# Loading the upper half of w_in's rows through GpSimd's DMA queue, with a new order of the opening steps

## The chip, the core and the metric

The kernel runs on one core of a Trainium2 chip. A core has five engines that work side by side, each through its own instructions in order: TensorE (PE, with its weight loads listed as PEld), VectorE (DVE), ScalarE (ACT), GpSimd (POOL) and SyncE (SP). SP computes nothing here; it issues DMAs, which bring data from memory into the on-chip buffer. ACT and POOL can issue DMAs as well. Sixteen DMA engines carry them out. The metric is the device time of one execution in microseconds (us).

## The reference

Two blocks follow each other. The first is a gated linear recurrence with a complex gate for 4 sequences of 768 steps and 8 heads of 48; the second is a two-layer network with an ELU between, on 3072 rows of 384 values and 2048 hidden ones. The weights come as float64, everything else as float32.

```python
mag = np.sqrt(a_re * a_re + a_im * a_im)
scale = np.minimum(mag, 0.999) / (mag + 1e-06)
a_re_n, a_im_n = (a_re * scale, a_im * scale)
for t in range(S):
    ar, ai = (a_re_n[:, :, t, :, None], a_im_n[:, :, t, :, None])
    new_re = ar * S_re - ai * S_im
    new_im = ar * S_im + ai * S_re
    kv = np.einsum('bhd,bhe->bhde', k[:, :, t], v[:, :, t])
    S_re, S_im = (new_re + kv, new_im)
    y[:, :, t] = np.einsum('bhd,bhde->bhe', q[:, :, t], S_re)
...
x = np.ascontiguousarray(attn_out.transpose(0, 2, 1, 3)).reshape(B * S, H * D)
h = x @ w_in
g = np.where(h > 0.0, h, alpha * (np.exp(np.minimum(h, 0.0)) - 1.0))
return (g @ w_out).astype(np.float32)
```

## The kernel before, in words

**Units.** The work is cut into 12 units (u = 0 to 11): 128 steps of two sequences each. A unit goes through the recurrence first, in these steps: the gate's magnitude and angle (`squares` or `squared`, `joined`, `logarithms`, `powers`, `lengths`, `ratios`, `slopes`, `angles`, on ACT and DVE), their sums along time as matmuls (`sums`, `summed`, `decays`, `turns`/`turned`), sines and cosines (`waves`, ACT), the scaling of q and k (`scaled`, `gated`, DVE), transposes on PE with copies on ACT (`transposed`), then `scores`, `states` and `values`, which are matmuls with DVE's masks and state sums and ACT's copies, `ends` (the decay over a whole block), and `seam`, a few small DMAs that move the last rows of the result into the layout of the second block. `noted` is an accuracy check on ACT whose outcome is only read at the very end. The second block then takes the unit as `inner` (x times w_in, two blocks of 128 hidden columns at a time, L1301), `elu` (ACT and DVE) and `project` (times w_out, L1326). Units 0 and 1 run through the plain products; later units use schemes with fewer products.

**Weights.** w_in and w_out stay on chip. Each comes in 8 parts of 768 KB of float64. `fetch` (L659 to 663) issues a part's DMAs on SP into a raw tile; `convert` takes one DVE step of rounding at a time from `rounded` (L665 to 683), four per part, w_in's eight parts first, then w_out's. A w_in part's rows lie on the 128 partitions in two halves: the rows of even heads on partitions 0 to 47 with a rest on 48 to 63, the rows of odd heads on 64 to 111 with a rest on 112 to 127. So a part of w_in is four DMAs (288, 288, 96 and 96 KB, in pieces of 2 KB), a part of w_out one (pieces of 3 KB). The raw tiles of w_in's parts 0 to 3 lie in memory that later holds the hidden values (tags g0 and g1), those of parts 4 to 7 and of all w_out parts in the two w64 buffers, which also hold unit 1's a, q and k. `inner(u, f)` needs part f/2 of w_in rounded, `project(u, n, f0, f1)` w_out's parts up to (f1 - 1)/2.

**Order.** The order of all steps is one list. Its first 329 entries are written out by hand (`first`, from L1745); the rest follows from a plan with due times (`put`, `layer_of`). Steps of the plan that `first` already holds are left out of it. Each step puts its instructions into the queues of the engines in this order, so the list sets every engine's order at once, SP's and POOL's DMA queues too: a DMA that must wait for a tile holds back every later one on its queue. `warm` issues dummy matmuls that keep PE's clock up. `table` loads one of ACT's function tables ahead of use; where a function is not in the table loaded, ACT loads another by itself (lines such as L832). The DMAs of a, q, k and v are at L607 and L611, those of the seam at L1281: for units 0 and 1 POOL issues those of the lower rows (unit 0's last on SP), ACT those of the upper ones (unit 0's last on SP). `carry_on` (L879) is a small DMA on POOL that hands a unit's last angle on; it waits for the turns.

**DVE's convert steps** (L671, L674, L677, L679): two cheap ones, two dearer.

Of the kernel before, what the change touches and what calls it, by code (L numbers as in the profile page):

```python
# [505 lines left out]
def kernel(  # L506
# [128 lines left out]
    def weights_of(kind, m):  # L635

        if kind == "in":
            n = WF * DM // NI
            dst, cols = w_in[:, :, ts(m, n)], ts(m, 2 * n)
            tag = "g" + str(m // 2) if m < 4 else "w64"  # L640
            t = sb.tile([C, WF * DM, 2], U32, tag=tag, bufs=2, name="w64")
# [1097 lines left out]
    def gates_of(u, *at):  # L1739
# [30 lines left out]
        (begun, 2), (squares, 2), (fetch, "out", 3), (joined, 2), (elu, 1, 6), *2 * [(convert,)], (elu, 1, 0), (convert,), (elu, 1, 2), *2 * [(convert,)], (elu, 1, 4),  # L1770
        (logarithms, 2), (inner, 1, 12), (load_a, 3), (convert,), (inner, 1, 8),
        (fetch, "out", 4), (inner, 0, 10), (inner, 0, 14), (elu, 1, 12), (inner, 0, 12), (convert,), (fetch, "out", 5), (convert,), (noted, 2), *2 * [(convert,)], (load_v, 2), (powers, 2),
        (elu, 1, 8), (convert,), (elu, 0, 10), (convert,), (ratios, 2),
        *2 * [(convert,)], (elu, 0, 14), (inner, 1, 10), *2 * [(convert,)], (elu, 0, 12),
        (convert,), (elu, 1, 10), *3 * [(convert,)], (load_qk, 2), (convert,), (fetch, "out", 6),
# [170 lines left out]
```

## Time and profile before

| what | value |
|---|---|
| median of 3 runs | 619.08 us (618.47 to 620.57) |
| profiled execution, its own time | 621.27 us |
| span of that execution, first to last instruction | 619.5 us |
| mean granted clock of PE | 0.997 |
| moved by DMA | 65.54 MB, of it q1 (SP's queue) 62.72 MB, q0 (POOL's) 1.20 MB |
| w_in's DMAs, issue to landing, median | 5.8 us (288 KB), 5.7 us (96 KB) |
| w_out's parts, issue to landing, median | 4.7 us (768 KB) |

The profile is a page on one execution. It lists the busy time of each engine, the span in 40 equal slices with the busy share of each in tenths, the DMA queues, and groups of instructions. A digit 9 is 90% or more. Further views of the same trace are used below: busy time of all engines in stretches of time, the waits of an engine by what ended them, and the instructions of one engine in order of time, where a bracket at the end gives the idle time before an instruction and what ended it. Several equal instructions in a row are merged into one line with their number, and then the duration is that of the group.

### The profile page before, as it was taken

What the parts mean: (1) busy time and instruction counts of PE and PEld (TensorE: products, weight loads), DVE (VectorE), ACT (ScalarE), POOL (GpSimd) and SP (SyncE); (2) the same over time, 40 slices, a digit from 0 to 9 for tenths busy, and PEclk for the clock granted to TensorE, in tenths of its full rate; (3) what the DMA queues carried; (4) which work ended last, traced back from release to release, by engine and by line L of the source; (5) the groups of instructions that cost most, each with busy time, mean ns of one, the idle gap of its engine ahead of it and who ended that gap; (6) DMA issues with size and microseconds to landing.
All of it is one profiled execution on the core that took longest, in us unless ns stands there. A gap on an engine that the chain in (4) does not pass through costs nothing. (4 is left out here: it accounts for less than half of the span.)

```text
span 619.5 us, 16960 instructions
## 1 busy us (share of the span) xinstructions
PE 605.0 (98%) x6980; PEld 550.0 (89%) x6980; DVE 503.0 (81%) x781; ACT 415.8 (67%) x681; POOL 176.5 (28%) x240
## 2 busy tenths in 40 slices
PE   8799999999999999999999999999999999999996
PEld 6678887567899999999999999999999999999996
DVE  5788878667599899888898898899898888984482
ACT  5975674675787667776777876777777777661350
POOL 2000100103113534523524434534534422422000
PEclk9989999999999999999999999999999999999999
DMA  9978739630653253746556545546673647342101
GB/s 165 183 139 136 152 111 239 145 65 22 91 90 58 53 97 81 143 95 123 118 104 123 118 103 121 125 99 122 126 134 85 142 80 132 73 87 66 53 2 32
DMA packets 192179, 65.54 MB, mean 106 GB/s; under 512 B 168116, under 2 KB 181596, under 8 KB 192092
## 3 DMA queue, kind: packets, MB, share of 16 engines
q1 hardware_dynamic: 187920, 62.72, 51.6%
q0 software_dynamic: 3520, 1.20, 1.7%
q8 instruction: 57, 0.93, 0.7%
q10 hardware_dynamic: 652, 0.44, 0.3%
q14 instruction: 30, 0.25, 0.2%
HBM read 48.91 MB, written 4.80 MB: 87 GB/s over the span
## 5 line engine op out<-in xcount | busy, mean ns | idle before, releaser
L1410 PE MATMUL mlp<-w_out,g 128*128 128x192 f32 x640 | 112.1, 328 | 0.0
L1410 PEld LDWEIGHTS mlp<-w_out,g 128*128 128x128 f32 x640 | 104.3, 190 | 3.3 <-DVE ee L1424 0.6
L1132 POOL TENSOR_TENSOR S<-S,T 128x384 f32<-128x384 f32 x36 | 38.0, 1057 | 150.0 <-DVE S L1130 83.1
L1388 DVE TENSOR_TENSOR g<-g 128x512 f32<-128x512 f32 x80 | 60.7, 774 | 6.3 <-PE mlp L1410 4.7
L1301 PE MATMUL mlp<-x,w_in 128*128 128x256 f32 x288 | 64.1, 381 | 0.0
L1301 PEld LDWEIGHTS mlp<-x,w_in 128*128 128x128 f32 x288 | 54.7, 192 | 8.5 <-issue 0.6
L1569 ACT ACTIVATE ee<-g 128x512 f32<-128x512 f32 x63 | 39.6, 629 | 29.5 <-DVE g L1564 26.8
L1548 PE MATMUL mlp<-x,w_in 128*128 128x128 f32 x424 | 56.3, 276 | 0.1
L1410 PE MATMUL mlp<-w,g 128*128 128x192 f32 x320 | 54.5, 329 | 0.0
L1410 PEld LDWEIGHTS mlp<-w,g 128*128 128x128 f32 x320 | 51.8, 190 | 0.6
L1548 PEld LDWEIGHTS mlp<-x,w_in 128*128 128x128 f32 x424 | 51.7, 192 | 0.6 <-DVE g L1564 0.3
L1281 POOL DMA_DIRECT2D x<-y x62 | 30.6, 499 | 72.2 <-ACT y L1177 40.4
L1570 ACT ACTIVATE ee<-ee 128x512 f32<-128x512 f32 x72 | 45.4, 631 | 2.3
L1573 DVE SCALAR_TENSOR_TENSOR g<-ee,g 128x512 f32<-128x512 f32 x63 | 42.4, 682 | 2.3 <-ACT ee L1570 2.3
L1561 ACT COPY g<-mlp 128x512 f32<-128x512 f32 x36 | 20.9, 584 | 29.4 <-PE mlp L1548 29.4
L1564 DVE TENSOR_TENSOR g<-g,mlp 128x512 f32<-128x512 f32 x45 | 30.8, 684 | 8.9 <-PE mlp L1548 4.1
L1291 ACT ACT_TABLE_LOAD x24 | 30.8, 1283 | 2.1 <-issue 1.6
L921 ACT ACTIVATE n<-w 64x384 f32<-64x384 f32 (+1 forms) x60 | 28.1, 486 | 5.2 <-PE w L906 4.4
L1548 PE MATMUL mlp<-x,g 128*128 128x128 f32 x224 | 30.1, 277 | 0.0
L1268 ACT COPY x<-y 128x384 f32<-128x384 f32 x20 | 8.6, 482 | 30.9 <-PE y L1160 30.9
L1075 POOL COPY qt<-kt 32x512 f32<-32x512 f32 x24 | 24.4, 1017 | 16.3 <-PE mlp L1548 10.2
L1548 PE MATMUL y<-x,w_in 128*128 128x128 f32 x216 | 28.5, 275 | 0.0
(218 smaller groups left out, 1369.7 us busy)
## 6 DMA issues: line engine op xcount, KB each, us to landing
w<-in_moe_w_out_dram SPq DMA_DIRECT2D x8, 768.0 KB, 4.7
g<-in_moe_w_in_dram SPq DMA_DIRECT2D x24, 256.0 KB, 3.1
g<-in_moe_w_out_dram SPq DMA_DIRECT2D x24, 256.0 KB, 3.0
w<-in_moe_w_in_dram SPq DMA_DIRECT2D x16, 288.0 KB, 5.8
vn<-in_v_dram SPq DMA_DIRECT2D x24, 192.0 KB, 5.6
qt<-kt SPq DMA_DIRECT2D x72, 64.0 KB, 2.0
kt<-cs SPq DMA_DIRECT2D x72, 64.0 KB, 2.3
q<-in_q_dram SPq DMA_DIRECT2D x11, 384.0 KB, 4.7
```

Of the source, the lines that this page charges most:

```text
L921: nc.scalar.activation(out=flat(x[key][to, n : n + 1]), in_=t[of], func=AF.Exp, scale=sign)
L1132: eng.tensor_tensor(out=new_s, in0=new_s, in1=wide, op=ALU.mult)
L1281: eng.dma_start(out=x["x"][ds(j * HP + D, G), i], in_=x["y"][ds(j * HP + i * G, G)])
L1291: nc.scalar.preload_act_table_set(name)
L1301: nc.tensor.matmul(t[:, e], lhsT=w_in[:, i, ts(f + e, C)], rhs=x["x"][:, i], start=(i == 0), stop=(i == NI - 1),)
L1388: nc.vector.tensor_tensor(out=S_of(u, k, h), in0=a, in1=b, op=op)
L1410: nc.tensor.matmul(to, lhsT=a[:, m], rhs=b[:, m], start=(first and h == 0 and m == 0), stop=False, skip_group_check=True,)
L1548: nc.tensor.matmul(x["c" + c][:, ts(m, C)], lhsT=a[:, m], rhs=x["mix"][p], start=(p == BANKS[c][0] and m == 0), stop=False, skip_group_che ...
L1564: nc.vector.tensor_tensor(out=part(u, to), in0=part(u, a), in1=part(u, b), op=op)
L1569: nc.scalar.activation(out=e, in_=part(u, of), func=AF.Relu, scale=-1.0)
L1570: nc.scalar.activation(out=e, in_=e, func=AF.Exp, scale=-1.0)
L1573: nc.vector.scalar_tensor_tensor(out=part(u, to), in0=nat[u]["e", to], scalar=-1.0, in1=part(u, of), op0=ALU.add, op1=ALU.max,)
```

## The change

It has three parts. The DMAs of w_in's upper rows (partitions 64 to 127) leave `fetch` and are issued by a new step, `fetch_far`, on POOL's queue. The raw tiles of w_in's parts 4 to 7 move from the w64 buffers into the tile of w_out, 4 blocks of 384 columns each, which holds nothing until the first part of w_out is rounded. And the written-out list is made anew: it has the same steps as often as before, the eight `fetch_far` steps besides, in another order. Of the list the diff shows here the beginning, as far as the first `inner` steps of unit 1.

```diff
@@ -637,8 +637,11 @@
         if kind == "in":
             n = WF * DM // NI
             dst, cols = w_in[:, :, ts(m, n)], ts(m, 2 * n)
-            tag = "g" + str(m // 2) if m < 4 else "w64"
-            t = sb.tile([C, WF * DM, 2], U32, tag=tag, bufs=2, name="w64")
+            if m < 4:
+                t = sb.tile([C, WF * DM, 2], U32, tag="g" + str(m // 2), bufs=2, name="w64")
+            else:
+                t = w_out[:, ts(m - 4, 2 * WF)].rearrange("p f n -> p (f n)").bitcast(U32)
+                t = t.rearrange("p (n two) -> p n two", two=2)
             words = t.rearrange("p (i n) two -> p i (n two)", i=NI)
             pairs = []
             for j in range(2):
@@ -658,13 +661,18 @@
 
     def fetch(kind, m):
         t, dst, pairs = weights_of(kind, m)
-        for to, of in pairs:
+        raw[kind, m] = t, dst, pairs[1::2]
+        for to, of in pairs[::2]:
             nc.sync.dma_start(out=to, in_=of)
-        raw[kind, m] = t, dst
+
+    def fetch_far(m):
+
+        for to, of in raw["in", m][2]:
+            nc.gpsimd.dma_start(out=to, in_=of)
 
     def rounded(kind, m):
 
-        w, dst = raw.pop((kind, m))
+        w, dst, _ = raw.pop((kind, m))
         lo, hi = w[:, :, 0], w[:, :, 1]
         f = sb.tile([C, WF * DM], U32, tag="wt", bufs=2, name="wf")
         r = sb.tile([C, WF * DM], U32, tag="wt", bufs=2, name="wr")
@@ -1743,54 +1751,68 @@
 
 
     first = [
-        (warm, 1), (warm, 12), (fetch, "in", 0), (begun, 0), (inverses, 0), (inverses, 1),
-        (load_qk, 0), (squared, "ar", 0), (squared, "ar", 1), (squared, "ai", 0),
-        (squared, "ai", 1), (joined, 0, 0), (logarithms, 0, 0), (joined, 0, 1), (logarithms, 0, 1),
-        (lengths, 0, 0), (ratios, 0, 0), (lengths, 0, 1), (powers, 0, 0), (sums, 1), (sums, 0),
-        (warm, 2), (powers, 0, 1), (ratios, 0, 1), *2 * [(convert,)], (table, "trig_and_small", 0),
-        (load_a, 1), (fetch, "in", 1), (load_v, 0), (angles, 0, 0), (fetch, "in", 2),
-        (angles, 0, 1), (summed, 0), (warm, 1), (decayed, 0, 0), (convert,), (summed, 1), (turned, 0, 0), (turned, 0, 1), (decayed, 0, 1), (waves, 0, 0), (waves, 0, 1),
-        (begun, 1), (table, "natural_log_exp_and_others", 0), (ends, 0), (scaled, 0, "q", 0),
-        (warm, 2), (warm, 1), (scaled, 0, "k", 0), (gated, 0, 0), (scaled, 0, "q", 1),
-        *2 * [(warm, 1)], (scaled, 0, "k", 1), (warm, 1), (squares, 1), (transposed, 0, "q", 0),
-        (transposed, 0, "k", 0), (convert,), (gated, 0, 1), (joined, 1), (transposed, 0, "q", 1),
-        *2 * [(convert,)], (load_qk, 1), (scores, 0, 0), (logarithms, 1), (states, 0, 0),
-        (powers, 1), (transposed, 0, "k", 1), (lengths, 1), (convert,), (ratios, 1), (convert,), (slopes, 1), (warm, 2), (noted, 1), (values, 0, 0), (decays, 1), (warm, 2), (scores, 0, 1),
-        (states, 0, 1), (angles, 1), *2 * [(warm, 2)], (scaled, 1), (noted, 0), (values, 0, 1),
-        (carry_on, 0), (fetch, "in", 3), (convert,), (ends, 1), (convert,), (seam, 0),
-        (load_v, 1), (table, "trig_and_small", 1), (convert,), (warm, 1), (turns, 1), (convert,), (waves, 1), (inner, 0, 2), (inner, 0, 0), (fetch, "in", 4), (load_a, 2), (fetch, "in", 5),
-        (table, "natural_log_exp_and_others", 1), (gated, 1, 0), (convert,), (gated, 1, 1),
-        (convert,), (elu, 0, 2), (transposed, 1, "q", 0), (transposed, 1, "k", 0),
-        (convert,), (transposed, 1, "q", 1), (scores, 1, 0), (convert,), (states, 1, 0),
-        (inner, 0, 4), *2 * [(convert,)], (transposed, 1, "k", 1), (convert,), (warm, 4),
-        (scores, 1, 1), (values, 1, 0), (fetch, "in", 6), (convert,), (fetch, "in", 7),
-        (states, 1, 1), (convert,), (elu, 0, 0), (convert,), (elu, 0, 4), (values, 1, 1),
-        (seam, 1), *2 * [(convert,)], (inner, 0, 8), (inner, 0, 6), (convert,), (elu, 0, 8),
-        (convert,), (inner, 1, 6), (inner, 1, 0), (fetch, "out", 0), (convert,), (inner, 1, 2), (elu, 0, 6), (convert,), (inner, 1, 4), (fetch, "out", 1), (fetch, "out", 2),
...
+        (begun, 0), (squared, "ar", 0), (squared, "ai", 0), (warm, 12), (joined, 0, 0),
+        (squared, "ar", 1), (squared, "ai", 1), (fetch, "in", 0), (load_qk, 0), (logarithms, 0, 0),
+        (inverses, 0), (ratios, 0, 0), (joined, 0, 1), (logarithms, 0, 1), (warm, 2), (inverses, 1),
+        (ratios, 0, 1), (fetch_far, 0), (lengths, 0, 1), (load_a, 1), (sums, 1), (angles, 0, 0),
+        (convert,), (angles, 0, 1), (lengths, 0, 0), (fetch, "in", 1), (powers, 0, 1), (convert,),
+        (powers, 0, 0), *2 * [(warm, 1)], (convert,), (turned, 0, 0), (turned, 0, 1), (load_v, 0),
+        (sums, 0), (begun, 1), (convert,), (warm, 2), (summed, 0), (fetch_far, 1), (decayed, 0, 0),
+        (summed, 1), (fetch, "in", 4), (decayed, 0, 1), (scaled, 0, "k", 0), (waves, 0, 0),
+        (scaled, 0, "q", 0), (warm, 1), (scaled, 0, "q", 1), (ends, 0), (waves, 0, 1),
+        (gated, 0, 0), (warm, 1), (begun, 2), (warm, 1), (scaled, 0, "k", 1), (warm, 1),
+        (squares, 1), (warm, 2), (gated, 0, 1), (transposed, 0, "q", 0), (fetch, "in", 2),
+        (load_qk, 1), (transposed, 0, "k", 0), (carry_on, 0), (transposed, 0, "q", 1), (convert,),
+        (joined, 1), (states, 0, 0), (convert,), (table, "natural_log_exp_and_others", 0),
+        (logarithms, 1), (convert,), (transposed, 0, "k", 1), (opened,), (convert,), (powers, 1),
+        (scores, 0, 0), (lengths, 1), (states, 0, 1), (warm, 2), (scores, 0, 1), (ratios, 1),
+        (fetch_far, 2), (noted, 1), (fetch, "in", 3), (convert,), (slopes, 1), (values, 0, 0),
+        (warm, 1), (decays, 1), (values, 0, 1), (table, "trig_and_small", 0), (warm, 2),
+        (fetch, "out", 0), (angles, 1), (seam, 0), (convert,), (ends, 1), (fetch, "in", 6),
+        (warm, 2), (scaled, 1), (turns, 1), (convert,), (load_qk, 2), (convert,), (waves, 1),
+        (gated, 1, 0), (load_v, 1), (fetch_far, 3), (inner, 0, 2), (inner, 0, 0), (fetch, "in", 5),
+        (elu, 0, 2), (transposed, 1, "q", 0), (gated, 1, 1), (transposed, 1, "k", 0),
+        (fetch_far, 4), (warm, 4), (load_a, 2), (fetch_far, 6), *2 * [(convert,)],
+        (transposed, 1, "q", 1), (begun, 3), (convert,), (scores, 1, 0), (states, 1, 0),
+        (fetch_far, 5), (inner, 0, 4), (convert,), (noted, 0), (convert,), (transposed, 1, "k", 1),
+        *2 * [(convert,)], (values, 1, 0), (convert,), (begun, 4), (elu, 0, 0),
+        (table, "natural_log_exp_and_others", 3), (scores, 1, 1), (squares, 2), (fetch, "in", 7),
+        *2 * [(convert,)], (states, 1, 1), (elu, 0, 4), (inner, 0, 8), (fetch_far, 7),
+        (values, 1, 1), (fetch, "out", 1), (joined, 2), (inner, 0, 6), (convert,), (seam, 1),
+        (inner, 1, 6), (convert,), (elu, 0, 8), (inner, 1, 0), (elu, 0, 6), *2 * [(convert,)],
...
```

In the rest of the new list, unit 2's gate steps come ahead of several of units 0 and 1's `inner` and `project` steps, and the last `convert` steps, the sums of weights for the later scheme (`combined`, `summed_in`) and unit 3's steps stand in a new order. `opened`, which only names buffers, stands much earlier.

More of the change, by code (lines that the diff above doesn't have):

```diff
@@ L1772 @@
[L1772 to L1775, printed above, removed]
-        (project, 1, 0, 0, 4), (convert,), (inner, 1, 14), (slopes, 2), *2 * [(convert,)], (project, 1, 1, 0, 4), (project, 0, 0, 0, 4), (angles, 2), (lengths, 2), (fetch, "out", 7),
@@ L1777 @@
-        (project, 0, 0, 4, 8), (elu, 1, 14), (project, 0, 1, 0, 4), (convert,), (decays, 2),
-        (project, 1, 0, 4, 8), (carried, 2), (convert,), (table, "trig_and_small", 2),
-        *2 * [(convert,)], (turns, 2), (waves, 2), (convert,), (table, "natural_log_exp_and_others", 2), (scaled, 2), (project, 0, 1, 4, 8), (convert,), (begun, 3), (table, "trig_and_small", 3), (project, 0, 1, 8, 12), (convert,), (project, 1, 1, 4, 8), (squares, 3), (gated, 2), (project, 1, 0, 8, 12), *2 * [(convert,)], (joined, 3), (convert,), (transposed, 2, "k", 1), (transposed, 2, "q", 1), (table, "natural_log_exp_and_others", 3), (convert,), (ends, 2), (convert,), (logarithms, 3), (project, 1, 1, 8, 12), (powers, 3), (load_qk, 3), (transposed, 2, "k", 0),
@@ L1780 @@
-        (convert,), (ratios, 3), (convert,), (lengths, 3), (project, 1, 0, 12, 16), (slopes, 3),
-        (transposed, 2, "q", 0), (project, 1, 1, 12, 16), (angles, 3), (scored, 2),
-        (opened,), (states, 2, 0), (valued, 2), *3 * [(convert,)], (seam, 2),
-        (project, 0, 0, 8, 12), (combined, 1, 1), (summed_in, 0), (noted, 3), (carried, 3),
-        (summed_in, 1), (combined, 2, 1), (combined, 4, 1), (combined, 1, 0), (summed_in, 4),
-        (summed_in, 2), (project, 0, 1, 12, 16), (combined, 2, 0), (turns, 3), (combined, 4, 0),
@@ L1786 @@
-        (inner, 2, 4), (inner, 2, 6), (load_a, 4), (ends, 3), (inner, 2, 2), (load_v, 3),
-        (inner, 2, 0), (elu, 2, 4), (scaled, 3), (elu, 2, 6), (summed_in, 3), (elu, 2, 2),
-        (waves, 3), (gated, 3, None, ("k",)), (elu, 2, 0), (gated, 3, None, ("q",)),
-        (project, 0, 0, 12, 16), (inner, 2, 10), (transposed, 3, "k", 0), (warm, 2), (begun, 4),
-        (folded, 2, 0, (3, 1)), (load_v, 4), (inner, 2, 8), (summed_in, 7), (squares, 4),
-        (elu, 2, 10), (load_qk, 4), (transposed, 3, "q", 0), (transposed, 3, "q", 1),
@@ new lines @@
+        (inner, 1, 6), (convert,), (elu, 0, 8), (inner, 1, 0), (elu, 0, 6), *2 * [(convert,)],
+        (load_a, 3), (convert,), (inner, 1, 2), (logarithms, 2), (convert,), (powers, 2),
+        (elu, 1, 6), (convert,), (inner, 1, 4), (convert,), (inner, 1, 12), (elu, 1, 0),
+        (inner, 1, 8), (ratios, 2), (elu, 1, 2), (convert,),
+        (table, "natural_log_exp_and_others", 1), (lengths, 2), (noted, 2), *2 * [(convert,)],
+        (elu, 1, 12), (elu, 1, 4), (slopes, 2), *2 * [(convert,)], (fetch, "out", 2), (convert,),
@@ new lines @@
+        (inner, 0, 14), (elu, 1, 8), (load_v, 2), *2 * [(convert,)], (inner, 0, 10), (angles, 2),
+        (convert,), (fetch, "out", 3), (elu, 0, 14), (convert,), (decays, 2), (inner, 0, 12),
+        (convert,), (fetch, "out", 4), (inner, 1, 14), (fetch, "out", 5), (project, 1, 0, 0, 4),
+        (carried, 2), (scaled, 2), (elu, 0, 10), *5 * [(convert,)], (squares, 3), (fetch, "out", 6),
+        *2 * [(convert,)], (ends, 2), (joined, 3), (turns, 2), (project, 1, 1, 0, 4),
+        *2 * [(convert,)], (fetch, "out", 7), (table, "natural_log_exp_and_others", 2),
@@ new lines @@
+        *2 * [(convert,)], (inner, 1, 10), (convert,), (elu, 1, 10), (logarithms, 3), (convert,),
+        (elu, 0, 12), (convert,), (waves, 2), (load_v, 3), (convert,), (project, 1, 1, 4, 8),
+        (gated, 2), (convert,), (project, 1, 0, 4, 8), (table, "trig_and_small", 2), (convert,),
+        (elu, 1, 14), (project, 0, 0, 0, 4), (project, 0, 1, 0, 4), (convert,),
+        (transposed, 2, "k", 1), (convert,), (project, 0, 1, 4, 8), (convert,),
+        (transposed, 2, "q", 1), (convert,), (transposed, 2, "k", 0), (convert,), (combined, 1, 0),
@@ new lines @@
+        (project, 1, 0, 8, 12), (summed_in, 1), (powers, 3), (ratios, 3), (convert,),
+        (project, 0, 1, 8, 12), (convert,), (slopes, 3), (project, 1, 0, 12, 16), (summed_in, 0),
+        (transposed, 2, "q", 0), (project, 1, 1, 8, 12), (noted, 3), (load_a, 4),
+        (project, 1, 1, 12, 16), (lengths, 3), (load_qk, 3), (angles, 3), (convert,), (scored, 2),
+        (project, 0, 1, 12, 16), (states, 2, 0), (valued, 2), (seam, 2), (load_v, 4), (carried, 3),
+        (project, 0, 0, 4, 8), (turns, 3), (inner, 2, 6), (inner, 2, 4), (inner, 2, 0), (elu, 2, 6),
@@ new lines @@
+        (elu, 2, 4), (scaled, 3), (waves, 3), (project, 0, 0, 8, 12), (summed_in, 3),
+        (combined, 2, 0), (combined, 4, 0), (elu, 2, 0), (gated, 3, None, ("q",)), (ends, 3),
+        (convert,), (project, 0, 0, 12, 16), (squares, 4), (gated, 3, None, ("k",)),
+        (combined, 3, 0), (inner, 2, 2), (inner, 2, 8), (table, "trig_and_small", 3), (warm, 2),
+        (summed_in, 4), (load_qk, 4), (elu, 2, 2), (combined, 1, 1), (transposed, 3, "k", 0),
+        (summed_in, 6), (convert,), (combined, 2, 1), (summed_in, 2), (inner, 2, 10),
@@ L1794 @@
+        (combined, 4, 1), (table, "trig_and_small", 1), (summed_in, 5), (transposed, 3, "q", 0),
+        (inner, 2, 12), (folded, 2, 0, (3, 1)), (elu, 2, 10), (convert,), (combined, 3, 1),
+        (transposed, 3, "q", 1), (summed_in, 8), (joined, 4), (elu, 2, 8), (transposed, 3, "k", 1),
+        (summed_in, 7),
     ]
```

4 lines of the change are left out of this document (removed).

## The prediction

> **What bounds the kernel now.** I read the profile's page first, then busy time by stretches, then what TensorE (PE) waited for.
>
> ```profile
> span 619.5 us, 16960 instructions
> PE 605.0 (98%) x6980; PEld 550.0 (89%) x6980; DVE 503.0 (81%) x781; ACT 415.8 (67%) x681; POOL 176.5 (28%) x240
> ...
> PE   8799999999999999999999999999999999999996
> ```
> ```profile
> 0.00:65.00 65.00, 57.94 (x778) 48.47 (x778) 49.26 (x74) 47.32 (x87) 5.92 (x34) 0.97 0.94 153
> 65.00:140.00 75.00, 75.00 (x395) 55.22 (x392) 57.44 (x78) 48.37 (x78) 4.06 (x6) 1.00 0.63 144
> ```
> ```profile
> 42.00:44.00 2.00, 2.00 (x5) 1.39 (x6) 1.61 (x3) 1.36 (x2) 0.00 (x0) 0.50 0.65 130
> ```
> ```profile
> PE w L1034 <- ACT qt L1038: 1.8, 1, 1.8
> PE mlp L889 <- DVE n L793: 1.1, 1, 1.1
> PE w L970 <- DVE once L968: 0.7, 2, 0.4
> PE w L963 <- ACT n L937: 0.7, 1, 0.7
> ```
>
> In the stretch rows the columns are PE, weight loads, DVE, ACT, POOL, then the granted PE clock, the DMA share and GB/s. PE bounds the kernel: 605.0 of 619.5 us. Of the 14.5 us in which it idles, 65.00 - 57.94 = 7.1 lie in the first 65 us, none between 65 and 140. The list that the change makes anew governs this opening. It holds the same steps as before with the same number of dummy matmuls (37 in both; I counted), so PE's work is the same and the change can only move PE's waits and the stretch at half clock (0.50 between 42 and 44). There is no line of a DMA among PE's longest waits: the opening is a chain through ACT and DVE, where DMA is a supplier that has so far been in time. What can be won is at most the waits after the first loads, some 5 us, and the half-clock stretch; what can be lost has no such cap.
>
> **ACT's queue.** In these rows the columns are start, duration, engine, line, operation.
>
> ```profile
> 21.37 1.28 ACT L1291 ACT_TABLE_LOAD   x1
> ...
> 35.44 1.28 ACT L832 ACT_TABLE_LOAD   x1
> ...
> 37.48 0.92 ACT L816 ACTIVATE n<-n,most_sq 128x768 f32<-128x768 f32 x1
> ...
> 39.46 0.72 ACT L1172 COPY x<-y 128x192 f32<-128x192 f32 x2
> ...
> 40.45 1.50 ACTq L1281 DMA_DIRECT2D x<-y  x2
> 41.98 1.28 ACT L1291 ACT_TABLE_LOAD   x1 [1.56 <-issue]
> 43.91 0.58 ACT L859 ACTIVATE n<-w,magic 128x384 f32<-128x384 f32 x1 [0.64 <-PE w L854]
> ```
>
> Unit 0's chain up to its waves has in both lists the same ACT steps and two table loads in it; angles now come ahead of powers, which swaps the loads and adds none. I let it end at 21.37 as before. Then, before: a load (1.28), 12.8 us of work up to 35.44 (squares to decays of unit 1), a load for the angles, the angles (36.72 to 37.48), noted(0) from 37.48 to 39.46, the copies of values(0, 1) 1.0, two DMA issues 1.5, another load, and the turns' first step at 43.91. New: the load moves behind squares and three pairs of copies but stays in the stretch: 21.4 + 1.3 + 12.8 = 35.5; copies 1.0, one load that serves angles and waves, 1.28: ACT is ready for the angles at 37.8. Gone from this stretch are noted(0), 2.0, which the new list puts behind states(1, 0), and one load, 1.28.
>
> **DVE's queue**, which must finish slopes(1) ahead of those angles.
>
> ```profile
> 23.14 0.95 DVE L679 SCALAR_TENSOR_TENSOR w_in<-w,wf 128x768 uint32<-128x768 uint32 x1
> ...
> 24.88 0.96 DVE L1020 TENSOR_TENSOR kg<-k,cs 128x768 f32<-128x768 f32 x1
> ...
> 26.62 0.56 DVE L671 TENSOR_SCALAR wr<-w 128x768 uint32<-128x768 uint32 x1
> ...
> 29.40 0.56 DVE L1128 TENSOR_TENSOR S<-mlp,T 128x384 f32<-128x384 f32 x1 [1.14 <-PE mlp L1115]
> ...
> 34.73 0.95 DVE L679 SCALAR_TENSOR_TENSOR w_in<-w,wf 128x768 uint32<-128x768 uint32 x1
> 35.60 0.95 DVE L807 SCALAR_TENSOR_TENSOR n<-n 128x768 f32<-128x768 f32 x1
> 36.47 0.68 DVE L1087 TENSOR_TENSOR a<-w,mask 128x512 f32<-128x512 f32 x1
> 37.23 0.56 DVE L1128 TENSOR_TENSOR S<-mlp,T 128x384 f32<-128x384 f32 x1
> ```
>
> Full tiles follow each other by 0.87 (34.73, 35.60, 36.47), cheap convert steps cost about 0.5. Before, gated(0, 1) ended at 24.88 + 0.87 = 25.8. The new list does part 0's last convert step (the row at 23.14) earlier, in an idle stretch, so 24.9. From there to the end of slopes(1) it has: part 1's four convert steps 2.8, one of part 2 0.5, joined, lengths and slopes 3 x 0.87 = 2.6, ratios 1.8, two masks 2 x 0.6, two sets of three state sums 2 x 1.7, and the wait for PE's state products, 1.2 as in the row at 29.40: 13.5, so 38.4. Before it was 36.47: scores(0, 1), states(0, 1) and a convert step now stand ahead of it. So angles(1) runs from 38.4 instead of 36.7, but behind it ACT has only the two DMA issues: 38.4 + 0.75 + 1.5 = 40.7, and with some 0.5 for the handovers the turns' first step at 41.2, 2.7 earlier than 43.91.
>
> **PE, and what then is late.**
>
> ```profile
> 42.38 2.77 PE L854 MATMUL w<-n,sum_turns 128*128 128x384 f32 x4
> 44.95 5.59 PE L1301 MATMUL mlp<-x,w_in 128*128 128x256 f32 x24
> ...
> 54.27 1.15 PE L1115 MATMUL w<-vn,kg 64*64 64x48 f32 x64
> ...
> 65.04 31.35 PE L1301 MATMUL mlp<-x,w_in 128*128 128x256 f32 x144
> ```
> ```profile
> x<-y ACTq DMA_DIRECT2D x2, 16.0 KB, 2.3
> ```
>
> The first inner(0, 2) follows the turns on PE directly before (44.95). In the new list the turns' matmuls are through at about 41, and inner(0, 2) needs unit 0's seam, whose last DMA ACT issues behind the angles, at about 40.2 to 41.2; with 2.3 to landing that is 43.5. So PE idles some 2.5 us on a DMA, a wait that is not there now, and starts 44.95 - 43.5 = 1.45 earlier. The 24 matmuls at 44.95 took 5.59 where the rate of the row at 65.04 gives 24 x 0.218 = 5.2: 0.4 of half clock, which I count as gone here. From there to states(1, 0) I find no new PE wait on ACT or DVE. The four dummy matmuls move ahead of it (0.9), neither gain nor loss in the end. Part 3 to 7's conversions stand with as much PE work ahead of their users as before, and noted(0), now at about 55, waits there beside long inner steps, where ACT has room; without that cover it would cost its 2.0. Between 65 and 140 PE never waited, so steps moved within that stretch count nothing; DVE's 57.44 of 75 us is the cover.
>
> Whether the clock falls again is open. The Trainium skill, page "TensorE: Matmul & The Clock Gate", section on the HAM clock gate, has it fall to half after an idle window of about 3.4 us, by which 2.5 us would not do it. The trace disagrees: the clock was at 0.50 from 42 on with no wait of PE longer than 1.8. So I bound it: a stretch of the same length at the new wait costs nothing against before; none gains up to 1.7 (3.4 us at half speed, an estimate from the row of 42 to 44); a second one loses 1.7. I take the middle.
>
> **The fetches.**
>
> ```profile
> 1.93 1.85 SPq L607 DMA_DIRECT2D ai<-in_a_im_dram  x2
> ...
> 41.72 1.38 SPq L607 DMA_DIRECT2D vn<-in_v_dram  x2
> ```
> ```profile
> 4.42 0.14 POOL L1625 MEMSET seen<- 128x60 f32 x1
> ```
> ```profile
> L974 POOL DMA_DIRECT2D T<-ends x20: 938/954/1002, 119.5 to 533.5; - x20
> ```
> ```profile
> vn<-in_v_dram SPq DMA_DIRECT2D x2, 192.0 KB, 4.5
> ```
> ```profile
> 10.00:20.00 10.00, 7.85 (x60) 5.44 (x59) 5.76 (x15) 9.49 (x16) 0.65 (x1) 1.00 1.34 188
> ```
> ```profile
> DMA packets 412, 0.75 MB, mean 186 GB/s; under 512 B 48, under 2 KB 48, under 8 KB 412
> ...
> q1 hardware_dynamic: 412, 0.75, 93.7%
> ```
> ```profile
> DMA packets 260, 0.75 MB, mean 300 GB/s; under 512 B 16, under 2 KB 16, under 8 KB 260
> ...
> q1 hardware_dynamic: 260, 0.75, 74.9%
> ```
>
> The last two pairs are 70 to 74 us, when w_in's halves were moving, and 75.5 to 78, with w_out's 128-row tiles: 0.75 MB cost 4.0 x 0.937 = 3.7 us of all engines for w_in and 2.5 x 0.749 = 1.9 for w_out. A w_in half of 384 KB thus holds the engines 2.0 us when sent alone, and 1.0 if halves sent together reach w_out's pace. The Trainium skill, page "DMA: Bandwidth & Descriptors", section "Rules for kernel authors", says of two transfers to disjoint partition halves: don't bother, they serialize; by it a half stays at 2.0. The rows above show w_in's slow pace but no two halves together.
>
> On SP each fetch loses two of its four issues. On POOL a fetch_far is two issues of at most 0.95 each (the row of L974, its dearest). Parts 0 and 1 wait for nothing and go out once POOL's set-up ends (4.42), when ai's issue is over (3.8): they can hold up a, q, k by 0 to 2 x 2.0 = 4.0, less the 2.0 that SP's own queue lost; I take 0. Parts 3 to 7 stand behind seam(0) and the carry of turns(1) on POOL, so they go out from about 43.5 on, five halves within some 6 us. Beside them SP loads unit 1's v, which the new list puts behind part 6's lower half and unit 2's q and k. Before, v went out at 41.72 and landed by 46.2, 8 us before states(1, 0) at 54.27. New: SP is free of the seam some 2.6 earlier, but ahead of v stand 2.0 and 786 KB at 188 GB/s = 4.2, so 49.8 alone; needed at 54.27 - 1.45 - 0.4 + 0.9 = 53.3. A margin of 3.5 against 1.0 to 2.0 for each half that gets in front: I take 0.3 for it, since only some do.
>
> **Sum**: -1.45 - 0.4 + 0.3 = -1.5 of the span of 619.5; the profiled execution's own 621.27 goes to 619.8, and as the median of the runs stands 2.2 under it, 617.6.
>
> **Rivals.** 1. *The opening shrinks by more*: the seam lands before the turns are through, so all 2.7 of the earlier turns count, and the half-clock stretch vanishes: -2.7 - 1.7 - 0.3 = -4.7, 614.4. For it: ACT loses 3.3 us of steps; against it: DVE's slopes come 2 us later. 2. *Slower, through unit 1's v*: nothing holds POOL's five halves back and they take the engines ahead of v, 5 to 10 us. It costs from 3.5 on; at five halves and 1.5 each v comes 4.0 late, PE stands at states(1, 0) (inner(0, 4) and all else queued behind), and the sum is -1.8 + 4.0 = +2.2, 621.3; at 2.0 each 623.7. That is where the skill's rule on halves would lead. Against it: SP's share of the engines goes on beside POOL's. 3. *No effect*: the wait for the seam brings a longer half-clock stretch that eats 1.7: 619.2.
>
> **Numbers.** Forecast 0.42, rival 1 0.20, rival 2 0.22, rival 3 0.16. About 0.3% (1.9 us) is what a measurement can tell from no change. The forecast lies just inside it and goes out to either side of that line by its unknown terms, half of it each: faster 0.20 + 0.21 = 0.41; slower the most of rival 2 and a little of 3, 0.23; the same 0.36. The range, 614.6 to 621.4, runs from rival 1 to rival 2's middle.
>
> **What would show it.** Right: ACT's turns step near 41 and one table load fewer before it; PE waiting 2 to 3 us for x's DMA ahead of L1301 near 43.5; the long run of L1301 shifted by 1 to 2 us. Rival 2: a PE wait of over 2 us at L1115 near 54 whose releaser is vn's DMA. Rival 1: no wait ahead of L1301. Wrong altogether: PE waits between 65 and 140, or DVE waiting for a raw part.

## The result and the profile after

The new kernel is slower: 635.79 us as the median of 4 runs (634.97 to 641.03) beside 619.83 us for the kernel before on the same chip (4 runs, 618.47 to 621.16). The ratio is 1.0272, with a 95% interval from 1.022 to 1.0324. The forecast was 617.6 with a range from 614.6 to 621.4. One execution of e5 below took 2168.23 us, the other five 624.83 to 632.81; that one is left out there, as of a slow state.

The page of the new kernel, in the rows that the prediction showed of the old one, with the granted clock and the DMA share by slices added; below it the clock of the kernel before:

```profile
span 634.2 us, 16962 instructions
PE 610.9 (96%) x6980; PEld 553.7 (87%) x6980; DVE 502.3 (79%) x781; ACT 423.7 (67%) x686; POOL 186.7 (29%) x256
...
PE   7798699999999999999999999999999999999996
...
PEclk9889699999999999999999999999999999999999
DMA  9989906637230334853945646646656656242101
```
```profile
PEclk9989999999999999999999999999999999999999
```

The span grew by 14.7 us (the profiled execution of the kernel before was one of 621.27 us, 2.2 above its median, so the medians differ by 16.0). PE idles 634.2 - 610.9 = 23.3 instead of 14.5, so 8.8 are new waits. The other 5.9 are PE's busy time (610.9 against 605.0) for the same 6980 matmuls, and the PEclk row tells why: it drops in the 2nd, 3rd and 5th slice, where the kernel before had a drop in the 3rd alone. Nearly all of both lies in the first five slices of 16 us: 8.2 of the 8.8 us of waits stand before 140 us.

Busy time by stretches (PE, weight loads, DVE, ACT, POOL, granted PE clock, DMA share, GB/s), first the two that the prediction showed, then one cut out:

```profile
0.00:65.00 65.00, 54.77 (x586) 45.81 (x586) 45.36 (x68) 43.21 (x77) 14.61 (x50) 0.95 1.07 166
65.00:140.00 75.00, 69.94 (x457) 52.86 (x455) 59.71 (x82) 52.13 (x82) 4.09 (x6) 0.93 0.55 124
```
```profile
69.20:79.20 10.00, 6.72 (x82) 5.50 (x79) 3.90 (x7) 5.07 (x7) 0.00 (x0) 0.50 1.02 196
```

Where PE never waited before (65 to 140) it now idles 5.1 us, and up to 65 it idles 3.2 more. The second fence holds the longest of three stretches at half clock (0.50): 10 us, in which PE was busy for 6.72 with work worth half of that. The other two, of 3.4 us each, begin at about 21.3 and 31.6. Together that is 17.1 us at half clock, where the profile before has 3.4.

PE's waits in the first 320 us, longest sums first (in total, times, longest):

```profile
PE mlp L1123 <- DMA vn<-in_v_dram: 3.0, 1, 3.0
PE w L1123 <- DMA vn<-in_v_dram: 2.4, 2, 1.3
PE w L1123 <- issue: 2.2, 1, 2.2
...
PE y L1159 <- issue: 1.8, 1, 1.8
```

The list before had no DMA in it; now one stands on top. v is late twice, once for unit 0 and once for unit 1. The chain of waits between 18 and 82 us shows how late (start, duration, what):

```profile
20.56 9.24 DMA vn<-in_v_dram
...
51.69 18.85 DMA vn<-in_v_dram
...
70.67 1.96 PE w L1123 x62
72.63 2.16 issue
```

Before, unit 0's v had landed 7.5 us after its issue and unit 1's 4.5; now it took 9.24 and 18.85. What stood beside the second one is in GpSimd's timeline, five upper halves within 8 us, and in the DMA rows of the wait itself, 51.7 to 70.5 us (packets, MB, share):

```profile
50.23 1.14 POOL L671 DMA_DIRECT2D w<-in_moe_w_in_dram  x2
51.36 2.76 POOL L671 DMA_DIRECT2D w_out<-in_moe_w_in_dram  x5
...
56.92 1.21 POOL L671 DMA_DIRECT2D w_out<-in_moe_w_in_dram  x2 [1.65 <-DMA w<-in_moe_w_in_dram]
```
```profile
q0 software_dynamic: 752, 1.97, 64.8%
q1 hardware_dynamic: 4213, 1.14, 50.1%
```

q0 is GpSimd's queue and q1 SP's. The percentages are the share that a queue's packets take of all 16 engines' time: 64.8 + 50.1 = 115, no room is left. GpSimd's 1.97 MB are all five halves (5 x 384 KB): every one of them moved while the second of v's two DMAs was under way. (18.85 - 4.5) / 5 = 2.9 us is what each upper half cost v, if the whole delay is theirs; by the time of the engines that they took it is 0.648 x 18.8 / 5 = 2.4.

Was the room there before? The DMA share answers it, and this is the reading that the prediction lacked. First three stretches of the kernel before, then the same of the new one:

```profile
8.00:20.00 12.00, 9.85 (x66) 6.55 (x65) 7.04 (x16) 10.47 (x18) 0.65 (x1) 1.00 1.30 186
20.00:30.00 10.00, 7.67 (x104) 6.70 (x103) 8.82 (x14) 9.94 (x16) 0.00 (x0) 1.00 1.11 181
30.00:40.00 10.00, 9.75 (x193) 8.29 (x191) 9.65 (x14) 9.80 (x23) 0.00 (x0) 1.00 0.97 152
```
```profile
8.00:20.00 12.00, 9.74 (x65) 6.50 (x63) 7.90 (x14) 9.36 (x16) 1.60 (x3) 1.00 1.28 172
20.00:30.00 10.00, 6.16 (x39) 5.68 (x40) 6.29 (x11) 9.25 (x16) 0.00 (x0) 0.83 1.20 182
30.00:40.00 10.00, 10.00 (x184) 9.10 (x186) 7.65 (x13) 5.46 (x10) 0.00 (x0) 0.83 1.02 158
```

The share sums the time that packets are under way on the 16 engines; packets of one engine overlap, so it can pass 1. In the kernel before it stands at about 1 or more from 8 to 40 us: the engines always held work, and the loads were still in time; that this rests on SP's one queue, which sends them in the order of need, is what e2 below tests. The second queue moved no more per second: 186, 181, 152 GB/s before, 172, 182, 158 after, and 182, 186, 181 with the new list on one queue (e1 below).

### The profile page after: what moved, and what is told of

Same layout as the page of the kernel before. It is cut to its first block, busy times and chain, and to the rows that moved or that the text cites. A ratio compares the mean times of both kernels' runs of the same rounds, so it can differ in the third digit from the quotient of the medians.

```text
span 634.2 us, 16962 instructions
## 1 busy us (share of the span) xinstructions
PE 610.9 (96%) x6980; PEld 553.7 (87%) x6980; DVE 502.3 (79%) x781; ACT 423.7 (67%) x686; POOL 186.7 (29%) x256
## 4 chain that ended last, share of the span: by engine, by line
PE 84%; DMA 7%; SPq 4%; DVE 3%; issue 1%; ACT 1%; DVEq 0%; ACTq 0%
PE mlp L1418 27%; PE mlp L1556 15%; PE mlp L1309 9%; PE y L1556 8%; DMA vn<-in_v_dram 4%; PE w L1123 4%; PE mlp L1334 3%; PE y L1334 3%; PE y L1168 3%; PE y L1238 3%; SPq L611 2%; PE y L1159 2%; PE w L862 2%; PE w L1042 1%; PE w L914 1%
## 5 line engine op out<-in xcount | busy, mean ns | idle before, releaser
L1309 PE MATMUL mlp<-x,w_in 128*128 128x256 f32 x288 | 67.2, 390 | 0.9 <-DMA x<-y 0.7
L1138 DVE TENSOR_TENSOR S<-w,S 128x384 f32<-128x384 f32 x38 | 20.9, 553 | 15.8 <-PE w L1123 14.5
L1123 PEld LDWEIGHTS w<-vn,kg 64*64 64x64 f32 x1280 | 23.5, 139 | 8.6 <-issue 5.9
L1123 PE MATMUL w<-vn,kg 64*64 64x48 f32 x1280 | 26.2, 225 | 4.6 <-DMA vn<-in_v_dram 2.4
L1320 DVE SCALAR_TENSOR_TENSOR g<-ee,mlp 128x512 f32<-128x512 f32 x24 | 16.4, 684 | 16.8 <-ACT ee L1319 16.8
```

Of the source, the lines that this page charges most:

```text
L1123: nc.tensor.matmul(to, lhsT=of, rhs=vn[u % 2][ts(c, L), n, ts(h, D)], start=True, stop=True,)
L1309: nc.tensor.matmul(t[:, e], lhsT=w_in[:, i, ts(f + e, C)], rhs=x["x"][:, i], start=(i == 0), stop=(i == NI - 1),)
```

## The experiments

Two theories. **Engines full**: w_in's narrow halves keep all DMA engines busy in the opening; a second queue adds no speed, only takes the order away, so something needed sooner lands later. **New list**: the new order of the compute steps is itself the harm, and the queue is a side matter. The runs compare with medians of the kernel before on their own chips: 620.32 (e1 to e4), 619.08 (e5 to e8) and 619.47 us (e9 to e12).

**e1, the new list on one queue.**

```diff
-        raw[kind, m] = t, dst, pairs[1::2]
-        for to, of in pairs[::2]:
+        raw[kind, m] = t, dst, []
+        for to, of in pairs:
```


> The new list and the raw tiles in w_out stay; each fetch issues all four DMAs of a part on SP again and the far steps issue nothing. Queue theory (POOL's halves take the DMA engines from a, v and the instruction loads): the waits for vn's DMA and for instructions shrink and most of the 14.7 us of span comes back, under 624 us. List theory (the new list itself puts too much to load ahead of v): unit 0's v still has parts 0, 1 and 4 ahead of it, now whole ones on the same queue, so the wait at states(0, 0) stays at 3 us or grows, and the time stays at 632 or more.

Measured: 629.02 us, ratio 1.0156 [1.0135, 1.0176]. So the queue is worth 635.79 - 629.02 = 6.8 on this list, and 8.7 remain. Both theories have a share, and the time lies between what either expected. v is nearly in time here (PE waits 0.2 for it), but the seams are not: SP issues the last DMAs of unit 0's seam behind its loads, and this issue takes 4.63 us. The first row is from PE's waits, of which two, 2.9 in all, stand at unit 0's seam and one, 2.3, at unit 1's; the second is from SP's timeline.

```profile
PE mlp L1309 <- DMA x<-y: 5.2, 3, 2.3
```
```profile
41.12 4.63 SPq L1289 DMA_DIRECT2D x<-y  x2
```

**e2, the old list with the second queue**, the upper halves issued on GpSimd where `fetch` stands; raw tiles as before.

```diff
-        for to, of in pairs:
-            nc.sync.dma_start(out=to, in_=of)
+        for n, (to, of) in enumerate(pairs):
+            eng = nc.gpsimd if n % 2 else nc.sync
+            eng.dma_start(out=to, in_=of)
```


> The list and the raw tiles of before; of each w_in part the two DMAs of the upper rows go out on POOL's queue at the place of the fetch. Queue theory: the old opening, which never waits for a DMA after the first loads, gets such waits: 5 us or more slower than before. List theory: it stays within 2 us of before. If halves on two queues really moved side by side, parts would land earlier and the time would not rise at all.

Measured: 638.15 us, 1.0321 [1.0283, 1.0359]: 18 us for the queue alone. PE's waits, ACT's wait, and GpSimd's timeline:

```profile
PE mlp L1302 <- DMA x<-y: 6.0, 1, 6.0
PE w L1035 <- ACT qt L1039: 5.6, 1, 5.6
PE w L1035 <- DVE qg L1021: 2.4, 1, 2.4
```
```profile
27.37 0.84 ACT L737 ACTIVATE n<-w 128x768 f32<-128x768 f32 x1 [5.09 <-DMA w<-in_a_re_dram]
```
```profile
4.51 3.45 POOL L663 DMA_DIRECT2D w<-in_moe_w_in_dram  x6
...
75.06 0.59 POOL L663 DMA_DIRECT2D w<-in_moe_w_in_dram  x1 [5.43 <-DVE w_in L680]
76.67 1.55 POOL L1282 DMA_DIRECT2D x<-y  x3
```

Two things happen. At 4.5 us GpSimd sends the upper halves of parts 0, 1 and 2 at once, while SP still has q, k and unit 1's a to send; a lands late, ACT's squares wait 5.09, and PE waits for ACT's copies, which stand behind the squares on ACT's queue. Later GpSimd itself stands 5.43 us for a raw buffer that DVE's conversion must free, and the seam of unit 1 is queued behind that: PE's 6.0.

**e3, the raw tiles in w_out alone**, old list, one queue.

```diff
-            tag = "g" + str(m // 2) if m < 4 else "w64"
-            t = sb.tile([C, WF * DM, 2], U32, tag=tag, bufs=2, name="w64")
+            if m < 4:
+                t = sb.tile([C, WF * DM, 2], U32, tag="g" + str(m // 2), bufs=2, name="w64")
+            else:
+                t = w_out[:, ts(m - 4, 2 * WF)].rearrange("p f n -> p (f n)").bitcast(U32)
+                t = t.rearrange("p (n two) -> p n two", two=2)
```


> The list and the one queue of before; only the raw tiles of parts 4 to 7 lie in w_out's unused space. All theories: SP waits less for buffers (21.8 us before) and PE waits as before, so within 1.5 us of before. If this place of the raw tiles costs something by itself, it shows here alone.

Measured: 620.39 us (10 runs), 1.0011 [0.9984, 1.0039]. This part costs nothing.

**e4, v ahead of the loads it waited behind**, in the new kernel.

```diff
-(load_a, 1), (sums, 1)
+(load_a, 1), (load_v, 0), (sums, 1)
...
-(convert,), (load_qk, 2), (convert,), (waves, 1),
+(convert,), (load_v, 1), (load_qk, 2), (convert,), (waves, 1),
```


> The changed kernel with only the v loads of units 0 and 1 moved up in the list: unit 0's directly behind unit 1's a, unit 1's ahead of unit 2's q and k. If the late v is what costs, PE's waits for vn (3.0, 1.3 and 1.1 us) go, and with them part of the half-clock time: 5 to 9 us less than the changed kernel, 627 to 631. If the engines are simply short of time in the opening, the waits move to the next loads (part 1, unit 1's q and k) and the time stays within 2 us of 635.8.

Measured: 638.28 us, 1.0321 [1.0286, 1.0357]. v's waits are gone, and PE idles 635.7 - 617.7 = 18.0 us, 5.3 less than in the new kernel. But its busy time rose by 6.8, from 610.9 to 617.7, which takes more than that away; the first row is the page's, the second PE's longest wait:

```profile
PE 617.7 (97%) x6980; PEld 557.8 (88%) x6980; DVE 502.0 (79%) x781; ACT 423.5 (67%) x686; POOL 187.0 (29%) x256
```
```profile
PE y L1159 <- issue: 3.0, 1, 3.0
```

The clock stands at half for 30.7 us in this profile, 17.1 in the new kernel's. So the waits did not simply move to other loads, as the second case of the expectation had it: 5.3 us of waits were won, and lost again to the clock. Why the clock falls more often here is not shown.

A wait whose releaser is "issue" has no cause in the profile. The two longest of the new kernel (1.8 and 2.2, between 65 and 75 us) lie where the DMA share is above 1, and e9 below, with half-free engines, has one of 1.0 alone; but another of 1.3 at 159 us lies in a stretch with a share of 0.33. Loads of instructions, which the page lists as DMA queues of their own, may be the cause; that is argued, not shown.

**e5, the new compute order with SP's loads in their old order**, one queue.

```diff
+(load_a, 1), (fetch, "in", 1), (load_v, 0), (fetch, "in", 2),
...
+(transposed, 0, "q", 0), (load_qk, 1), (fetch, "in", 3),
...
+(seam, 0), (load_v, 1),
...
+(waves, 1), (fetch, "in", 4),
...
+(elu, 0, 2), (fetch, "in", 5),
...
+(inner, 0, 4), (fetch, "in", 6),
```


> The changed kernel's order of the computing steps, with one queue, and with the loads on SP put back into the order of before (unit 1's v ahead of part 4, unit 2's q and k and w_out's first part behind w_in's last). If the new list's 8.7 us on one queue come from the loads that it moves forward, this is at 620 or less, and the 1.5 us that I worked out for the order of the computing steps show as 617 to 619. If the order of the computing steps itself is worse, it stays at 625 or more.

Measured: 627.69 us as the median of five, 1.0155 [1.0118, 1.0191], as e1. Another order of loads on one queue does not bring the new list back. PE waits 3.2 for unit 1's seam, issued while w_in's parts 6 and 7 (1.5 MB) fill the engines.

**e6, the old list with the second queue for parts 0 to 2 only.**

```diff
+            eng = nc.gpsimd if n % 2 and m < 3 else nc.sync
```


> The list of before; only parts 0, 1 and 2 have their upper halves on POOL's queue, parts 3 to 7 stay on SP whole. Theory of running ahead (POOL's first halves have nothing to wait for and take 2.6 us of all DMA engines each, ahead of q, k and unit 1's a): ACT waits some 5 us for unit 1's a and the time is 626 to 630. The rest of the 18 us then belongs to POOL's own order: the seam of unit 1 behind a fetch that waits for its buffer (6.0 us). Rival: any use of POOL's queue costs by its descriptors, in which case the cost goes by the number of halves, 3 of 8, some 7 us, but as waits for parts of w_in and not for a.

Measured: 625.41 us, 1.013 [1.0099, 1.0162]. PE's longest waits are the early ones of e2, smaller: 3.0 for ACT's copies and 1.9 for DVE's qg, none for a part of w_in. So of e2's 18 us, 6.3 come from the three halves that run ahead and, if the two sums simply add, some 12 from the five later ones.

**e7, the new list on one queue with wide loads**: one DMA per part over all 128 partitions. In e7 and in e9 to e11 the rows of w_in lie in another order on the partitions, so the first product of the second block takes wrong rows: their output is not the reference's, and only their times are used.

```diff
-            pairs = []
-            for j in range(2):
-                heads = ...
-                pairs.append((words[ds(j * HP, D)], heads[j]))
...
+            pairs = [(words, moe_w_in[:, cols].rearrange("(i p) n -> p i n", i=NI))]
```


> The new list on one queue, each part of w_in as one DMA over all 128 partitions in the same pieces of 2 KB; w_in's rows then lie in another order on the partitions, so the product uses the wrong rows of it. If it is the narrow set of partitions that makes w_in slow (165 ns a piece), a piece goes down to 85 to 100 ns, a part takes 2 us of all engines and not 4, and the new list's DMA waits shrink: 620 to 624 against 629.0. If the 2 KB pieces or the reading from memory are slow, pieces stay at 160 ns or more and the time at 628 or more.

Measured: 622.65 us, 1.0065 [1.005, 1.008]: of the 8.7 us that the new list cost on one queue, 3.6 are left. Its stretches, to be read against the kernel before's above, and the first inner step, for which the prediction had set a time:

```profile
8.00:20.00 12.00, 9.64 (x66) 6.67 (x64) 8.66 (x16) 10.40 (x18) 0.65 (x1) 1.00 1.34 231
20.00:30.00 10.00, 10.00 (x112) 9.30 (x114) 7.55 (x12) 9.06 (x16) 0.00 (x0) 0.83 1.03 256
30.00:40.00 10.00, 9.78 (x206) 8.22 (x204) 9.45 (x15) 8.98 (x21) 1.09 (x2) 1.00 0.31 95
```
```profile
43.53 6.02 PE L1303 MATMUL mlp<-x,w_in 128*128 128x256 f32 x24 [0.22 <-DMA x<-y]
```

The loads move at 231 and 256 GB/s, where e1 with the same list had 182 and 186, and from 30 to 40 us the DMA share is 0.31, where e1 had 1.04. In the new kernel itself that inner step came 5.2 later:

```profile
48.72 0.67 PE L1309 MATMUL mlp<-x,w_in 128*128 128x256 f32 x2 [0.71 <-DMA x<-y]
```

**e8, the old list with both other parts** (e2's and e3's edits together).

> The list of before with both other parts of the change: upper halves on POOL's queue and the raw tiles of parts 4 to 7 in w_out. POOL's fetches no longer wait for buffers, so unit 1's seam is not held up behind them: the 6.0 us wait for x goes, and of the 18 us some 10 to 12 stay, 630 to 632. If the seam's wait comes from full DMA engines, it stays near 638.

Measured: 640.25 us, 1.0346 [1.0331, 1.0361], not the 630 to 632 expected. The raw tiles in w_out did take away the wait for the seam, since GpSimd no longer stands for a buffer: there is no wait of PE for x. But then no buffer holds its halves back, and PE waits elsewhere, for ACT's copies as in e2 and twice with no releaser (4.3 and 2.9). The clock stands at half for 30.7 us.

```profile
PE w L1038 <- ACT qt L1042: 4.9, 1, 4.9
PE w L1119 <- issue: 4.3, 1, 4.3
```

**e9, e10 and e11, wide loads with the other combinations of list and queue.** The wide part on two queues is four DMAs again:

```diff
+            rows = moe_w_in[:, cols].rearrange("(i p) n -> p i n", i=NI)
+            pairs = [
+                (words[:, 0], rows[:, 0]), (words[:, 2], rows[:, 2]),
+                (words[0 : C // 2, 1], rows[0 : C // 2, 1]), (words[C // 2 : C, 1], rows[C // 2 : C, 1]),
+            ]
```


> The new kernel with both queues, at the new list's places, but with w_in's rows laid on all 128 partitions: SP carries the first third of the rows (256 KB over 128 partitions) and half of the second, GpSimd the last third and the other half, so each queue has as many DMAs and bytes as in the new kernel (the rows stand in another order on the partitions, so the first product of the second block takes wrong rows). Theory 'the engines are full': with pieces that move twice as fast the second queue has little to overtake, and the time comes to 622 to 625, near the one-queue kernel with such rows (622.65). Rival 'the second queue harms by its lack of order, full engines or not': the difference between the new kernel and the new list on one queue (635.8 - 629.0 = 6.8) stays, and the time is 628 to 631.

> The kernel before, with each part of w_in loaded by one DMA over all 128 partitions (rows in another order, so the first product of the second block takes wrong rows). Theory 'in the kernel before the narrow loads are already hidden, its PE never waits for one': 618 to 620, no change. Rival 'the narrow loads cost the kernel before as well': 614 to 617, as ACT and DVE get q, k and v earlier.

> The old list on two queues (the upper shares issued by GpSimd where fetch stands), with rows on all 128 partitions as in the run on the new list. Theory 'the engines are full': the 18 us that the same split cost with narrow halves shrink to 0 to 5, 619 to 624. Rival 'lack of order harms by itself': GpSimd's queue still sends the shares of parts 0 to 2 at once, ahead of a, q and k, and most of the 18 us stay, 630 to 638.

Measured: e9 622.46 us, 1.0056 [1.0035, 1.0077]; e10 619.09, 0.9998 [0.9985, 1.001]; e11 626.68, 1.0125 [1.0103, 1.0146]. With e7, e1, e2, before and after this makes a table of medians:

| | one queue | two queues |
|---|---|---|
| old list, narrow halves | 619.5 | 638.15 |
| old list, wide loads | 619.09 | 626.68 |
| new list, narrow halves | 629.02 | 635.79 |
| new list, wide loads | 622.65 | 622.46 |

With wide loads the second queue costs nothing on the new list, where it cost 6.8, and 7.6 instead of 18 on the old one. (The new list has its raw tiles in w_out, the old one in the table does not; e3 and e8 show what that place does on the old list: nothing on one queue, 2 us more on two.) The stretch of 55 to 75 us, in which the new kernel's five halves met v, shows it; first the new kernel, then e9:

```profile
55.00:75.00 20.00, 13.65 (x288) 12.18 (x286) 12.79 (x20) 10.25 (x20) 1.37 (x3) 0.85 1.11 162
```
```profile
55.00:75.00 20.00, 19.16 (x268) 16.17 (x261) 16.33 (x25) 13.93 (x28) 1.46 (x3) 1.00 0.57 138
```

Same list, as many issues and bytes on the same queues: with the engines half free PE is busy for 19.16 of 20 us, with full ones for 13.65. What is left in e11 is one long wait, with 6.8 us more at half clock than e10, and it is e2's second: GpSimd's fetch stands for a raw buffer with the seam behind it. GpSimd's rows, then PE's:

```profile
59.93 1.10 POOL L661 DMA_DIRECT2D w<-in_moe_w_in_dram  x2 [9.38 <-DVE w_in L678]
66.46 0.57 POOL L661 DMA_DIRECT2D w<-in_moe_w_in_dram  x1 [5.43 <-DVE w_in L678]
...
67.94 1.46 POOL L1280 DMA_DIRECT2D x<-y  x3
```
```profile
71.85 23.37 PE L1300 MATMUL mlp<-x,w_in 128*128 128x256 f32 x96 [4.85 <-DMA x<-y]
```

So of the 16 us, 6.8 are the second queue's and go with wide loads; of the 8.7 that the new list costs on one queue, 5.1 go with them too. And e10 says that the kernel before gains nothing from faster loads: on its one ordered queue the narrow loads are hidden.

**e12, the old list on two queues, held in order**: GpSimd copies an element of the lower rows of a part before it sends the upper ones.

```diff
+            s = sb.tile([G + D, 1], U32, tag="seen_raw", bufs=2, name="seen_raw")
+            nc.gpsimd.tensor_copy(out=s, in_=t[0 : G + D, 0, 0:1])
+        for to, of in pairs[1::2]:
+            nc.gpsimd.dma_start(out=to, in_=of)
```


> The old list on two queues with the narrow halves, but GpSimd copies one element of the lower half's rows of a part (partitions 0 to 63) before it issues the upper half, so that an upper half goes out only when the lower one has landed: it can't overtake what SP's list has ahead of its part. Theory 'overtaking is the harm': most of the 18 us go, 620 to 627. Rival 'GpSimd's queue takes the engines' time, whenever it sends': 632 to 639 as before. A third outcome is possible: GpSimd's own small DMAs of the seam stand behind these waits, and the cost goes there, 625 to 632, with PE waiting for x's DMA.

Measured: 642.66 us, 1.0365 [1.0341, 1.0389]. The third outcome of the expectation had named the place, the seam behind GpSimd's waits, but not the size. The upper half of part 0 now goes out only at 10.70, so the part comes late to DVE, whose queue stands 7.92 us before its first conversion (the profile names no releaser) with unit 0's work behind it; and GpSimd's seam of unit 1 stands behind its copies until 85.62, for which PE waits 9.2:

```profile
18.91 0.56 DVE L676 TENSOR_SCALAR wr<-w 128x768 uint32<-128x768 uint32 x1 [7.92 <-issue]
```
```profile
PE mlp L1306 <- DMA x<-y: 9.6, 2, 9.2
```

It brought a wait of its own, so it does not tell whether overtaking alone is the harm. The table does that better: the same places of issue with quicker loads.

## Why the prediction was wrong

**What bounds the kernel** was right as far as it went: PE, and an opening that governs all. But the sentence "DMA is a supplier that has so far been in time" took being in time for having room. The prediction's own row of 10 to 20 us had a DMA share of 1.34, and it was not used.

**The step that failed** is, in the sum, the term for the fetches, +0.3. The same list is 6.8 us quicker with all loads on SP (e1). It failed in two places. First, the early far halves "can hold up a, q, k by 0 to 2 x 2.0 = 4.0 [...]; I take 0". They did hold things up: of unit 0's v, which this sentence does not even name, PE waited 3.0 (0.2 in e1). Second, v of unit 1: "I take 0.3 for it, since only some do". All five halves got in front, at 2.4 to 2.9 us each where the bound was 2.0, and v landed after 18.85 us instead of 4.5.

Two more terms were wrong. The order of the computing steps was to win 1.45 + 0.4; on one queue the new list costs 8.7 instead (e1), 3.6 with quick loads (e7). And the clock, taken as no change, cost up to 6.8. Both are taken up below.

Both signs that the prediction had named for "wrong altogether" are there: PE waits between 65 and 140, and DVE waited 5.4 us in two waits for raw parts of w_in (1.1 before).

```profile
DVE wr L679 <- DMA w<-in_moe_w_in_dram: 5.4, 2, 3.4
```

**Rival 2** had this mechanism, with its place, and named the right condition ("nothing holds POOL's five halves back"). Its sign, a PE wait of over 2 us for unit 1's v, came only in pieces: 1.3 and 1.1. It was priced at 621.3 to 623.7 against 635.8, for three reasons: 1.5 to 2.0 instead of 2.4 to 2.9 for a half, one victim where there were several (v twice, the seam, DVE's conversions), and the gains of the compute order still in its sum. (Three figures of the prediction are off without weight: 621.4, the range's upper end, is this rival's lower price and not its middle, 614.6 stands 0.2 above rival 1's 614.4, and the 0.95 us called the most for an issue is that row's median; these issues took 0.52 to 0.61.) The argument against it, "SP's share of the engines goes on beside POOL's", was true and useless: a share of full engines is a slower queue. The rule cited there, that two transfers to disjoint partition halves serialize (Trainium skill, "DMA: Bandwidth & Descriptors", "Rules for kernel authors"), agrees with the runs: from 20 to 30 us 182 GB/s with two queues against 186 on the same list with one (e1). Its section "SWDGE vs HWDGE vs iDMA" adds that an engine takes turns between the two kinds of queue; e2's late a fits that: the list orders each queue, not one against the other.

**The compute order** was met in its times where loads are quick, but it won nothing. ACT's turns step was forecast for 41.2 and ran at 42.07 in e7, the first inner step for 43.5 and ran at 43.53. (In the new kernel they came at 47.40 and 48.72.) The seam landed at 43.5 as forecast; the wait for it was 0.2 instead of 2.5, since PE's turns ran at half clock and were through only just before. What failed is what these times were compared with. The 44.95 of the kernel before is from one execution whose half-clock stretch lay on just this place, from 42 on. In the profiles of e3 and e10, with the old list on one queue, that stretch lies between 18 and 24, and the first inner step begins ahead of the new list's 43.53; the first row is e3's (narrow halves), the second e10's (wide loads):

```profile
42.45 5.49 PE L1304 MATMUL mlp<-x,w_in 128*128 128x256 f32 x24
```
```profile
42.68 5.34 PE L1295 MATMUL mlp<-x,w_in 128*128 128x256 f32 x24
```

So the 1.45 + 0.4 us were a gain over one unlucky execution and not over the kernel.

**The clock.** The prediction bounded its effect between a gain and a loss of 1.7 and took the middle, nothing. There were three stretches instead of one, 3.4 + 3.4 + 10.2 us less the 3.4 of before, which is up to 6.8 lost at half speed; PE's longer busy time shows 5.9 of it. No single wait of PE passed 3.0 us, which again speaks against the idle window of about 3.4 us of the Trainium skill's page "TensorE: Matmul & The Clock Gate" (section on the HAM clock gate), if it means one unbroken wait.

**What stays open.** With wide loads the new list is 3.6 us slower than the old one (e7 against e10). The clock accounts for most or all of that: in the two profiles PE idles the same, 13.0 and 12.8 us, and is busy for 606.3 and 603.6. e7 has a second stretch at half clock, from 41 to 45 us, e10 one alone; over all executions the mean granted clock is 0.991 in e7 and 0.997 in e10, and 0.006 of 620 us is an estimate of 3.6. Why the new list brings the second stretch, and e4 and e8 nine times 3.4 us, no run shows. No version tried beats the kernel before.

## What to carry to other kernels

Before you give a load a second queue, read the DMA share of the stretch. At 1.0 to 1.3 a second queue brought no speed here and took away the order that one queue kept, and everything needed sooner than the moved load was a victim to be priced, not only the first. A landing time from a trace (4.5 us for v) holds only for the load of the engines at that place. A queue whose DMAs wait for buffers must not carry, behind them, small DMAs that the bound engine waits for (e2, e11). And before you count a gain against a time in a profile, look whether a stretch at half clock lies on it: another execution may have it elsewhere.

## What the hardware showed that was not expected

- **Narrow loads are slow**: where 768 KB parts went as four DMAs over 48 and 16 partitions, the stretches from 8 to 30 us ran at 182 and 186 GB/s (e1); as one over 128 partitions at 231 and 256 (e7). It is the width more than the number of DMAs: as four over 128 and 64 partitions they ran at 214 and 227 (e9). For PE of the kernel before that made no difference (e10).
- **An issue takes long while the engines are full.** SP's timeline in e2 has 0.43 us for the issue of q and 7.83 for that of unit 1's first a, both of 384 KB; in the kernel before the latter took 1.88. All that stands behind on SP is held up by it, and the seam's DMAs can take as long (4.63 in e1).

```profile
5.16 0.43 SPq L611 DMA_DIRECT2D q<-in_q_dram  x1
...
10.81 7.83 SPq L611 DMA_DIRECT2D w<-in_a_re_dram  x1
```
- **The clock falls in whole steps, and not in proportion to the waits.** In the first 200 us of every profile here the time at half clock is a multiple of 3.41 us: once that in the kernel before, e3, e6 and e10, twice in e7 and e9, three times in e1, e5 and e11, five in the new kernel and e2, seven in e12, nine in e4 and e8. PE idles 31.4 us in e12 and 18.0 in e4, yet e4 is longer at half clock.
